# Other engines and row order for the ends of two weight loads, keys issued ahead of x, and a split projection, in a one-token decode layer

## Chip, cores and metric

The kernel runs on one core of a Trainium2 chip. The metric is the device time of one execution in microseconds (us). Several runs are taken of each kernel. The kernel before takes 196.8 to 197.0 us, depending on the set of runs. Differences of one per cent matter here, so each experiment was timed against the kernel before on the same chip, in alternating rounds.

## The reference, cut to what matters

Eight tokens go through attention over a cache (8 key heads, the last 1024 positions) and through a small MLP. A gate mixes the two.

```python
x: (8, 1, 448)   k_cache, v_cache: (8, 8, 4096, 256), last 1024 positions used
wq: (448, 4096)  wo: (4096, 448)   w1: (448, 1792)   w2: (1792, 448)
g = sigmoid((x * gate_w).sum(-1))
a = attention(x @ wq, k[..., -1024:, :], v[..., -1024:, :]) @ wo
b = gelu(layernorm(x) @ w1 + b1) @ w2 + b2
out = g * a + (1 - g) * b
```

About 78 MB have to be read for very little arithmetic. The 448 rows of `wq` and `w1` are 384 rows, which fill 128 partitions three times, and an end of 64 rows.

## The kernel before

Everything large streams through a ring of nine slots of 128 x 8192 elements. All of these loads are issued by the SP engine, in the order of a plan: keys 0, `w1`, `wq`, `w2`, then keys and values in turn, last `wo`. There are 16 steps of keys and values. The last `wo` part is split into three loads.

```python
wq_m = A_wq[0:DM, :].rearrange("(p r) n -> p (r n)", r=NR)      # 128 partitions
wq_t = A_wq[DM:D, :].rearrange("r (h n) -> (r h) n", h=2)       # end: 128 half rows
w1_m = B_w1[0:DM, :].rearrange("(p r) f -> p (r f)", r=NR)
w1_t = B_w1[DM:D, :].rearrange("r (h n) -> (r h) n", h=2)       # end: 128 half rows
...
x_sb = consts.tile([NB, D], BF16)
nc.sync.dma_start(x_sb[:], xf)     # x first on SP's queue
pump()                             # then the first nine loads of the plan
...
# the last steps (u is the last of 16)
values(u - 1)
...
finish(u - 1)
values(u)          # 32 matmuls: weights times values
finish(u)          # transposes the result into oT
for i in range(HPQ):               # row spread: 16 small matmuls into pp
    for m in range(HPQ):
        nc.tensor.matmul(pp[32*i : 32*i + 32, m], lhsT=ident[:, m::HPQ], rhs=oTv[:, i], ...)
nc.vector.tensor_copy(oP[:], pp[:]...)
for q in range(NHQ):               # projection: 128 matmuls with wo
    ...
nc.vector.scalar_tensor_tensor(res[:], in0=A_ps[:], scalar=gg_s[:, 0:1], in1=mixb[:], ...)
for i, (src, cols) in enumerate(quads(res)):     # four output stores
    eng = nc.sync if i % 2 == 0 else nc.scalar
    eng.dma_start(out_f[:, cols], src)
```

## Time and profile before

| kernel before | value | where it is read |
|---|---|---|
| time | 196.85 us median of 6 (196.59 to 197.06) | runs |
| bytes loaded on SP's queue | 77.67 MB at about 427 GB/s | page, queues and slices |
| share of DMA in the chain that ended last | 96% | page, chain |
| keys of step 14 begin | 160.78 us | timeline |
| compute's part of the projection ends | 190.05 us (187.00 + 3.05) | timeline |
| last `wo` part lands | just before 190.27 us | timeline, wait |
| the span ends | 195.0 us | page |

First the page of the profile of before, cut: the granted clock, the DMA share and the rate in forty slices of the span, then the DMA queues, then the chain that ended last.

```profile
PEclk9997566999999999999999999999999999999655
DMA  4999999999999999999999999999999999999940
GB/s 165 426 425 408 444 421 427 408 424 424 430 424 430 420 430 427 427 427 424 425 424 430 427 427 417 425 424 424 417 424 430 427 430 420 427 424 407 413 151 3
...
q1 hardware_dynamic: 6528, 77.67, 94.7%
q8 instruction: 18, 0.29, 0.6%
...
q14 instruction: 4, 0.03, 0.0%
...
DMA 96%; SPq 1%; issue 0%; PE 0%; DVE 0%
```

A DMA digit of 9 in 37 slices on end says that the loads never pause. Queue q1 is SP's. Two queues are of the kind "instruction", which I read as the program itself being fetched: 18 packets of 16 KB on q8, of 1.01 to 1.11 us each, and four of 8 KB on q14. The page counts them as a share of the same sixteen engines (0.6% for q8).

Next the table of stretches of before. The columns are the stretch, its length, the busy time of each compute engine with its number of instructions, the granted clock, the DMA share and the rate.

```profile
core 0: us, PE busy (x) PEld busy (x) DVE busy (x) ACT busy (x) POOL busy (x), PEclk, DMA share, GB/s
20.00:25.00 5.00, 4.59 (x137) 4.51 (x137) 1.55 (x7) 0.30 (x1) 0.00 (x0) 0.50 1.07 449
185.00:187.00 2.00, 1.14 (x20) 0.98 (x19) 0.65 (x2) 0.00 (x0) 0.00 (x0) 0.50 0.60 233
187.00:189.00 2.00, 2.00 (x88) 2.00 (x92) 0.00 (x0) 0.00 (x0) 0.00 (x0) 0.50 0.41 151
189.00:191.00 2.00, 1.41 (x52) 0.89 (x40) 0.32 (x1) 0.00 (x0) 0.00 (x0) 0.50 0.06 17
```

The end is not clean. The DMA share falls to 0.60, 0.41 and 0.06 over six microseconds, because the sixteen DMA engines finish at different times. A full load has sixteen completions in the trace, which I take for one per engine. Those of the last `wo` load spread over 4.6 us: seven come from 185.05 to 185.70 us, one at 187.28, seven from 188.16 to 188.67, and the last at 189.65.

The last microseconds of before in the timeline (start, duration, engine, source line, operation, and the idle time before it with what ended it):

```profile
187.00 3.05 PE L562 MATMUL A_ps<-slot,oP 128*8 128x112 bf16 x120 [0.55 <-DVE oP L555]
190.27 0.36 PE L562 MATMUL A_ps<-slot,oP 128*8 128x112 bf16 x8 [0.22 <-DMA slot<-in_A_wo_dram]
...
190.68 0.33 DVE L569 SCALAR_TENSOR_TENSOR res<-A_ps,gg_s,mixb 128x112 bf16<-128x112 f32 x1 [3.73 <-PE A_ps L562]
191.04 1.05 SPq L579 DMA_DIRECT2D out_dram<-res  x2
191.04 0.67 ACTq L579 DMA_DIRECT2D out_dram<-res  x2
```

The 120 matmuls that have their data end at 190.05, and the last eight wait for `wo` until 190.27. So loads and compute end within 0.3 us of each other. After the last sum (the DVE line) come the output stores: SP takes 1.05 us to issue its two, ACT 0.67.

One further line of the timeline of before marks how far the stream is near the end: the keys of step 14, which wait for their load.

```profile
160.78 1.51 PE L322 MATMUL ktp<-ident,slot 128*128 128x128 bf16 x24 [0.55 <-DMA slot<-in_A_k_cache_dram]
```

### The profile page before, as it was taken

The numbers are of one execution on the slowest core, as the hardware profiler recorded it, in microseconds if no ns is written. First come the engines' busy times: TensorE is split into PE (matmuls) and PEld (weight loads), VectorE is DVE, ScalarE is ACT, GpSimd is POOL, SyncE is SP. The second block draws the span as 40 slices with busy tenths as digits, with TensorE's granted clock in tenths as the row PEclk, the third lists the DMA queues.
The fourth block names the chain that finished last, engine by engine and source line by source line (L and its number), as shares of the span: only waits on it lengthen the run. The fifth ranks groups of instructions, "written<-read, shape, count | busy, mean of one in ns | idle before, by whom it ended". The sixth has DMA issues, their size and how long they took to land.

```text
span 195.0 us, 5167 instructions
## 1 busy us (share of the span) xinstructions
PE 148.3 (76%) x2318; PEld 110.5 (57%) x2318; DVE 112.6 (58%) x258; ACT 82.9 (43%) x101; POOL 0.9 (0%) x7
## 2 busy tenths in 40 slices
PE   1399967887778787878767878778787878994780
PEld 0399927755565656564636464647373737553570
DVE  7531342867575757575738484847575757777210
ACT  2362003636373727272708181818282828562000
POOL 1000000000000000000000000000000000000000
PEclk9997566999999999999999999999999999999655
DMA  4999999999999999999999999999999999999940
GB/s 165 426 425 408 444 421 427 408 424 424 430 424 430 420 430 427 427 427 424 425 424 430 427 427 417 425 424 424 417 424 430 427 430 420 427 424 407 413 151 3
DMA packets 6744, 78.02 MB, mean 400 GB/s; under 512 B 945, under 2 KB 1346, under 8 KB 1986
## 3 DMA queue, kind: packets, MB, share of 16 engines
q1 hardware_dynamic: 6528, 77.67, 94.7%
q8 instruction: 18, 0.29, 0.6%
q10 hardware_dynamic: 194, 0.02, 0.1%
q14 instruction: 4, 0.03, 0.0%
HBM read 77.68 MB, written 0.01 MB: 398 GB/s over the span
## 4 chain that ended last, share of the span: by engine, by line
DMA 96%; SPq 1%; issue 0%; PE 0%; DVE 0%
DMA slot<-in_A_k_cache_dram 58%; DMA slot<-in_A_v_cache_dram 20%; DMA slot<-in_A_wo_dram 10%; DMA slot<-in_A_wq_dram 7%; SPq L107 1%; SPq L123 1%; PE A_ps L562 0%; SPq L172 0%; DVE res L569 0%
## 5 line engine op out<-in xcount | busy, mean ns | idle before, releaser
L325 ACT COPY kt<-ktp 128x1024 bf16<-128x1024 bf16 x64 | 63.2, 1017 | 82.1 <-PE ktp L322 82.1
L322 PE MATMUL ktp<-ident,slot 128*128 128x128 bf16 x1024 | 71.2, 226 | 21.6 <-ACT kt L325 10.9
L322 PEld LDWEIGHTS <-slot 128*128 128x128 bf16 x1024 | 64.8, 103 | 28.4 <-issue 15.6
L327 DVE COPY kt<-ktp 128x1024 bf16<-128x1024 bf16 x64 | 41.3, 685 | 16.0 <-PE ktp L322 16.0
L360 PE MATMUL S_ps<-kt,qw 128*8 128x512 bf16 x256 | 32.4, 627 | 0.3 <-DVE qw L351 0.3
L372 DVE TENSOR_REDUCE nmx<-S_ps 128x1 f32<-128x1024 f32 x16 | 19.6, 1225 | 22.4 <-PE S_ps L360 22.4
L388 DVE STREAM_TRANSPOSE EB<-E 128x1024 bf16<-128x1024 bf16 x16 | 19.9, 1245 | 6.3 <-ACT E L380 6.1
L420 PE MATMUL PO<-slot,ET 128*8 128x256 bf16 x512 | 17.6, 282 | 6.1 <-DVE ET L401 6.1
L380 ACT ACTIVATE E<-S_ps,nmx 128x1024 bf16<-128x1024 f32 x16 | 17.9, 1120 | 2.4 <-DVE nmx L373 2.4
L420 PEld LDWEIGHTS <-ET 128*8 128x8 bf16 x512 | 11.4, 88 | 10.3 <-DVE ET L401 8.4
L360 PEld LDWEIGHTS <-qw 128*8 128x8 bf16 x256 | 7.3, 95 | 12.0 <-issue 10.4
L401 DVE CAST ET<-sm 128x256 bf16<-128x256 f32 x16 | 6.7, 417 | 0.5 <-PE sm L399 0.5
L396 PE MATMUL sm<-EB,perm 128*128 128x256 bf16 x16 | 4.4, 273 | 1.6 <-DVE EB L388 1.6
L399 PE MATMUL sm<-selr,ones_f 128*128 128x8 f32 x32 | 5.3, 237 | 0.0
L440 DVE CAST oT<-sm 128x16 bf16<-128x16 f32 x16 | 3.5, 221 | 2.8 <-PE sm L437 2.8
L399 PEld LDWEIGHTS sm<-selr,ones_f 128*128 128x128 f32 x32 | 4.8, 188 | 0.1
L562 PE MATMUL A_ps<-slot,oP 128*8 128x112 bf16 x128 | 3.4, 295 | 0.8 <-DVE oP L555 0.5
L339 PE MATMUL qt<-xT,slot 128*128 128x8 bf16 x128 | 3.6, 168 | 0.4 <-DVE z L470 0.4
L339 PEld LDWEIGHTS <-slot 128*128 128x128 bf16 x128 | 3.6, 104 | 0.4 <-issue 0.3
L562 PEld LDWEIGHTS <-oP 128*8 128x8 bf16 x128 | 2.9, 121 | 1.2 <-DVE oP L555 0.7
L470 DVE TENSOR_TENSOR z<-hT,b_sb 128x112 f32<-128x112 f32 x1 | 0.3, 275 | 5.5 <-PE hT L460 5.5
L380 ACT ACTIVATION_READ_ACCUMULATOR E<-S_ps,nmx 128x1 f32 x16 | 3.2, 202 | 0.0
(122 smaller groups left out, 71.9 us busy)
## 6 DMA issues: line engine op xcount, KB each, us to landing
slot<-in_A_v_cache_dram SPq DMA_DIRECT2D x16, 2048.0 KB, 38.9
slot<-in_A_k_cache_dram SPq DMA_DIRECT2D x15, 2048.0 KB, 39.4
slot<-in_A_wo_dram SPq DMA_DIRECT2D x3, 896.0 KB, 32.0
slot<-in_A_k_cache_dram SPq DMA_DIRECT2D x2, 1024.0 KB, 7.1
slot<-in_A_wq_dram SPq DMA_DIRECT2D x1, 2048.0 KB
slot<-in_B_w_dram SPq DMA_DIRECT2D x1, 1568.0 KB
slot<-in_B_w_dram SPq DMA_DIRECT2D x1, 1344.0 KB, 9.8
slot<-in_A_wq_dram SPq DMA_DIRECT2D x1, 1024.0 KB
```

Source lines behind the costliest of these rows:

```text
L322: nc.tensor.transpose(ktp[:, c, :], kn[:, o : o + P], ident[:])
L325: nc.scalar.copy(dst, ktp[:])
L327: nc.vector.tensor_copy(dst, ktp[:])
L339: nc.tensor.matmul(qt[:, k, :], lhsT=w[:, o + c : o + c + P], rhs=xT[:, r + half, :], start=(r == 0 and k == 0), stop=(r == NR), skip_grou ...
L360: nc.tensor.matmul(S_ps[32 * a : 32 * a + RQ, hf * CH * SK : (hf + 1) * CH * SK], lhsT=qw[:, j, b, half, a, :], rhs=KT[hf][:, j, :, a::QUA ...
L372: nc.vector.reduce_max(nmx[:], S_ps[:], axis=AXIS.X, negate=True)
L380: nc.scalar.activation(E[:], S_ps[:], ACT.Exp, bias=nmx[:], scale=1.0, accum_out=rowsum[:])
L388: nc.vector.transpose(EB[:].rearrange("p c r -> p (c r)"), E[:])
L399: nc.tensor.matmul(sm[:, NCK, :], lhsT=ones_f[:], rhs=selr[:], start=True, stop=True)
L401: nc.vector.tensor_copy(ET[:], sm[:, 0:NCK, :])
L420: nc.tensor.matmul(PO[32 * t : 32 * t + RQ, :], lhsT=ET[:, c, 0:RQ], rhs=vn[:, c * Dh : (c + 1) * Dh], start=(c < QUAD), stop=(c >= NCK - ...
L562: nc.tensor.matmul(dst, lhsT=oP[:, j, q, :], rhs=w[:, o + cols.start : o + cols.stop], start=(q == 0 and j == 0), stop=(q == NHQ - 1 and j ...
```

## The change

Three edits in one:

1. The ends of `wq` (512 KB) and `w1` (224 KB) are loaded as 64 full rows in partitions 0 to 63, not as 128 half rows in 128 partitions. The source is viewed as eight groups of eight rows, each group backwards. The load then runs on eight DMA engines (the load queue of after has 720 four-byte packets, taken for completion writes, against 736 in the run no_tails below, which keeps the old ends: eight fewer for each of the two). That each engine has one group of the view is how I laid out this load; the trace has no engine numbers and does not show it. The intent is to even out the finish of the engines, and to need fewer matmuls.
2. `x` goes to ACT's queue, so that the first keys are the first thing on SP's queue.
3. The row spread is cut in halves. The first half, and with it a part of the projection's preparation, moves ahead of the last value step, and a quarter of the projection is done before the second half.

```diff
-    wq_t = A_wq[DM:D, :].rearrange("r (h n) -> (r h) n", h=2)
+    wq_t = A_wq[DM:D, :].rearrange("(e j) n -> e j n", j=TE)[:, ::-1, :]    # TE = 8
-    w1_t = B_w1[DM:D, :].rearrange("r (h n) -> (r h) n", h=2)
+    w1_t = B_w1[DM:D, :].rearrange("(e j) n -> e j n", j=TE)[:, ::-1, :]
... (loader: destination t[0:64]; xT, yT and the matmuls of the end follow)
-    nc.sync.dma_start(x_sb[:], xf)
     pump()
+    nc.scalar.dma_start(x_sb[:], xf)
...
-    values(u)
-    finish(u)
-    (row spread of all heads, then the projection)
+    spread_rows(0, HALF)
+    values(u)
+    finish(u)
+    project(0)
+    spread_rows(HALF, NHQ)
+    for q in range(1, NHQ):
+        project(q)
```

More of the change, by code (lines that the diff above doesn't have):

```diff
@@ L51 @@
     NF = F // P
-    FH = F // 2
-    HH = HD // 2
+    TE = DT // 8
     QUAD = 4
@@ L116, in load @@
             for ap in pieces:
-                n = 1
-                for s in ap.shape[1:]:
-                    n *= s
-                dst = t[:, o : o + n]
-                if len(ap.shape) == 3:
-                    dst = dst.rearrange("p (a n) -> p a n", a=ap.shape[1])
-                nc.sync.dma_start(dst, ap)
+                n = ap.shape[-1]
+                rows = 1
+                for s in ap.shape[:-1]:
+                    rows *= s
+                nc.sync.dma_start(t[0:rows, o : o + n], ap)
                 o += n
@@ L191 @@
     nc.vector.memset(PO[:], 0.0)
-    NX = NR + 2
+    NX = NR + 1
     DQ = D // QUAD
@@ L200, in quads @@
         ]
-    xz = consts.tile([NB, 2, P], BF16)
-    yz = consts.tile([NB, 2, P], BF16)
-    nc.vector.memset(xz[:], 0.0)
-    nc.vector.memset(yz[:], 0.0)
+    xz = consts.tile([NB, DT], BF16)
+    yz = consts.tile([NB, DT], BF16)
     xT = consts.tile([P, NX, NB], BF16)
@@ L223, in transposed @@
             nc.tensor.transpose(tp[:, r, :], src[:, r:DM:NR], ident[:NB, :NB])
-        for h in range(2):
-            nc.tensor.transpose(tp[:, NR + h, :], srcz[:, h, :], ident[:NB, :NB])
-        nc.vector.tensor_copy(dst[:], tp[:])
-    for h in range(2):
-        nc.vector.tensor_copy(xz[:, h, h::2], x_sb[:, DM:D])
+        nc.vector.tensor_copy(
+            srcz[:].rearrange("b (e j) -> b e j", j=TE),
+            src[:, DM:D].rearrange("b (e j) -> b e j", j=TE)[:, :, ::-1],
+        )
+        nc.tensor.transpose(tp[0:DT, NR, :], srcz[:], ident[:NB, :NB])
+        nc.vector.tensor_copy(dst[:, 0:NR, :], tp[:, 0:NR, :])
+        nc.vector.tensor_copy(dst[0:DT, NR, :], tp[0:DT, NR, :])
     transposed(xT, x_sb, xz)
@@ L270, in norm_and_gate @@
         )
-        for h in range(2):
-            nc.vector.tensor_copy(yz[:, h, h::2], y_sb[:, DM:D])
         transposed(yT, y_sb, yz)
@@ L335, in query @@
             w, o = slot("wq", r // 2), (r % 2) * HD
+            kp = P if r < NR else DT
             for k in range(Hq * NJ):
                 col = (k // NJ) * Dh + (k % NJ) * P
-                half, c = divmod(col, HH) if r == NR else (0, col)
                 nc.tensor.matmul(
                     qt[:, k, :],
-                    lhsT=w[:, o + c : o + c + P],
-                    rhs=xT[:, r + half, :],
+                    lhsT=w[0:kp, o + col : o + col + P],
+                    rhs=xT[0:kp, r, :],
                     start=(r == 0 and k == 0),
@@ L446, in mlp_hidden @@
         w = slot("w1")
-        for r in range(NR):
-            o = r * F
+        for r in range(NR + 1):
+            kp = P if r < NR else DT
             for c in range(NF):
@@ L451, in mlp_hidden @@
                     hT[:, c, :],
-                    lhsT=w[:, o + c : o + F : NF],
-                    rhs=yT[:, r, :],
+                    lhsT=w[0:kp, r * F + c : (r + 1) * F : NF],
+                    rhs=yT[0:kp, r, :],
                     start=(r == 0 and c == 0),
-                    stop=False,
-                    skip_group_check=True,
-                )
-        for h in range(2):
-            for c in range(NF):
-                nc.tensor.matmul(
-                    hT[64 * h : 64 * h + 64, c, :],
-                    lhsT=w[:, NR * F + c : NR * F + FH : NF],
-                    rhs=yT[:, NR + h, :],
-                    start=False,
-                    stop=True,
+                    stop=(r == NR),
                     skip_group_check=True,
@@ L539, with spread_rows, project @@
     finish(u - 1)
-    values(u)
-    finish(u)
-    pp = ps_sm.tile([P, HPQ, NJ, NHQ, NB], F32, tag="sm", name="pp")
+    oP = consts.tile([P, NJ8, NHQ, NB], BF16)
     oTv = oT[:].rearrange("p (q i) j b -> p i j q b", i=HPQ)
-    for i in range(HPQ):
-        for m in range(HPQ):
-            nc.tensor.matmul(
-                pp[32 * i : 32 * i + 32, m],
-                lhsT=ident[:, m::HPQ],
-                rhs=oTv[:, i],
-                start=True,
-                stop=True,
-            )
-    oP = consts.tile([P, NJ8, NHQ, NB], BF16)
-    nc.vector.tensor_copy(oP[:], pp[:].rearrange("p m j q b -> p (m j) q b"))
-    for q in range(NHQ):
+    def spread_rows(q0, q1):
+        pp = ps_kt.tile([P, HPQ, NJ, q1 - q0, NB], F32, tag="ktp", name="pp")
+        for i in range(HPQ):
+            for m in range(HPQ):
+                nc.tensor.matmul(
+                    pp[32 * i : 32 * i + 32, m],
+                    lhsT=ident[:, m::HPQ],
+                    rhs=oTv[:, i, :, q0:q1, :],
+                    start=True,
+                    stop=True,
+                )
+        nc.vector.tensor_copy(
+            oP[:, :, q0:q1, :], pp[:].rearrange("p m j q b -> p (m j) q b")
+        )
+    def project(q):
         w = slot("wo", q - q % 2)
@@ L568 @@
                 )
+    HALF = NHQ // 2
+    spread_rows(0, HALF)
[5 more added lines that the diff above has]
+        project(q)
     nc.vector.scalar_tensor_tensor(
```

## The prediction

> **What bounds it now.** The loads. In the page's 40 slices the DMA row is at 9 throughout, 77.67 MB at about 427 GB/s; the chain of waits gives 96% of the span to DMA. But the last 5 us are not clean. In the table of stretches the DMA share is 1.02 at 180-185 us, then 0.60, 0.41 and 0.06 in the next three 2 us: the 16 DMA engines stop at different times. The trace's packets of the load queue end at about 185.2 us on seven engines, 187.4 on one, 188.2 to 188.8 on seven and 189.8 on one. The 18 instruction packets of 16 KB (about 1.06 us each) fit this: two on each of eight late engines, a third on the last.[...]
>
> A second limit runs beside it. In the timeline, keys 14 start on DMA at 160.78, then PE, ACT and DVE work in series to the last value step (182.25), finish, row spread and projection (120 matmuls, 187.00-190.05). The last 8 matmuls wait for wo until 190.23. So loads and compute end within 0.2 us of each other.
>
> **What changes.**
> 1. The tails of wq (512 KB) and w1 (224 KB) go to eight engines, not sixteen.[...] Those eight get 46 KB more, the others 46 KB less: at 427/16 GB/s, 1.73 us each way (estimate). I take it that the light eight are the early finishers (about 85%; the trace carries no engine numbers). Then ends become 186.9 (seven), 189.1 (the one at 187.4), 186.9 (seven), 188.0.
> 2. First keys lead the load queue: x's issue (0.73 to about 1.17 us) leaves it, so loads start 0.44 us earlier. x on ACT's queue is not critical.
> 3. 14 fewer hidden-layer matmuls, 2 fewer transposes, two memsets less; off the critical path (keys 1 wait for DMA at 31.36 anyway).
> 4. Projection: half the row spread before the last value step (delays it about 0.7 us: the oT copy, then 16 small matmuls); the rest hides its copies (0.32 + 0.55 us of PE idle before) behind projection. PE works at clock 0.5 there, so net about 0.1 us.
>
> **Sum.** The last wo landing moves from 190.23 to about 189.2 (0.44 + 0.6). Keys 14: the engine that is 1.4 us early now becomes the last, so they land only 0.1 to 0.5 us earlier, and compute follows: projection ends near 189.8. It ended at 190.63. Gain about 0.8 us, up to 2.2 if the intermediate engine is in the relieved half[...].
>
> **Predicted: 196.0 us, range 194.6 to 197.3.** Faster by over 2%: 0.05; within 2%: 0.92; slower: 0.03.
>
> **Right or wrong shows so.** Tail DMA share stays near 1 until about 186.5, then drops in under 2.5 us; first key packets start 0.4 us earlier; the projection's last matmuls no longer wait for wo but follow PE; keys 14 start within 0.5 us of 160.5; no PE idle from the copies after the last value step.
>
> **What would make it wrong.**[...] Early stages may suffer while the overloaded engines lag (wq lands later; query at 21.4).[...] Refill packets falling on other engines move the last landing by 1 us.

The sum came to a gain of about 0.8 us, with the end of the projection going from 190.63 to about 189.8 us, and of up to 2.2 us; the second case for the 2.2 us is cut, and so is a clock term of 1 to 2 us under what would make it wrong. For the landing of the last `wo` part, 0.6 is an estimate from the ends of the engines and the 1.73 us of step 1. Eight engines: if they were the late finishers, the end would slip by 1.3 us, to 198 us (an estimate: 1.73 less 0.44). How the 18 instruction packets (the "refill packets" of the last line) fall on the engines, and that they move the last landing by 1 us, are estimates from their count and the 1.06 us of one.

## The result, and the profile after

| | before | after |
|---|---|---|
| time, median of 6 runs | 196.85 us | 198.91 us |
| range | 196.59 to 197.06 | 198.27 to 200.39 |

The ratio after to before is 1.0111, with a 95% interval of 1.0075 to 1.0148. Ratios are the mean time of one kernel's fast runs over that of the other's fast runs of the same rounds, so they are not quite the ratio of the medians. The profiled run of after has a span of 196.5 us, against 195.0.

The page of after, the same lines as for before where they exist:

```profile
PEclk9997558699999999999999999999999999999755
DMA  5999999999999999999999999999999999999950
GB/s 210 412 377 407 268 392 427 422 424 427 420 427 424 427 424 427 427 427 424 430 429 420 427 424 430 424 425 420 430 430 430 424 430 427 427 428 404 404 215 13
...
q1 hardware_dynamic: 6368, 77.67, 95.3%
q8 instruction: 18, 0.29, 0.6%
...
DMA 83%; PE 9%; ACT 3%; DVE 2%; issue 1%; SPq 1%; ACTq 0%
```

The fifth number of the rate row is 268 GB/s, where before has 444. The DMA row still says 9 there. The engines are busy, but they move little: each packet takes longer. A busy share alone would have hidden it.

The table of stretches of after:

```profile
core 0: us, PE busy (x) PEld busy (x) DVE busy (x) ACT busy (x) POOL busy (x), PEclk, DMA share, GB/s
20.00:25.00 5.00, 1.98 (x69) 1.81 (x65) 0.49 (x2) 0.27 (x1) 0.00 (x0) 0.50 1.05 256
185.00:187.00 2.00, 1.69 (x32) 1.67 (x36) 0.58 (x3) 0.00 (x0) 0.00 (x0) 0.50 0.93 383
187.00:189.00 2.00, 1.48 (x29) 0.94 (x19) 0.46 (x2) 0.00 (x0) 0.00 (x0) 0.50 0.88 345
189.00:191.00 2.00, 2.00 (x68) 1.98 (x72) 0.23 (x2) 0.00 (x0) 0.00 (x0) 0.50 0.27 106
```

From 20 to 25 us the DMA share is 1.05 and the rate 256 GB/s, against 1.07 and 449 before. Near the end the DMA share stays high up to 189 us, so the loads end later.

In the table of waits of after, lines stand that before does not have, with PE waiting for these loads (total, number of times, longest):

```profile
PE qt L334 <- DMA slot<-in_A_wq_dram: 4.2, 2, 3.2
...
PE PO L415 <- DMA slot<-in_A_v_cache_dram: 1.1, 1, 1.1
```

The timeline of after, keys 14:

```profile
164.52 1.51 PE L317 MATMUL ktp<-ident,slot 128*128 128x128 bf16 x24 [0.52 <-DMA slot<-in_A_k_cache_dram]
```

Keys 14 start 3.74 us later than before (164.52 against 160.78). Then the end:

```profile
190.54 0.34 PE L532 MATMUL pp<-oT,ident 128*32 128x32 bf16 x16
...
190.70 2.52 PE L548 MATMUL A_ps<-slot,oP 128*8 128x112 bf16 x96
...
193.27 0.33 DVE L565 SCALAR_TENSOR_TENSOR res<-A_ps,gg_s,mixb 128x112 bf16<-128x112 f32 x1 [1.98 <-PE A_ps L548]
193.63 0.67 SPq L575 DMA_DIRECT2D out_dram<-res  x2
```

From keys 14 to the last sum, after needs 28.75 us (193.27 - 164.52) and before 29.90 (190.68 - 160.78). The rearranged end is therefore quicker, and the output stores are too: from the start of the last sum to the end of the span it is 3.2 us (196.5 - 193.27), against 4.3 before. So after loses 3.7 us early and wins back 2.2 us late (1.15 before the last sum, 1.1 behind it).

The packets of the trace show what was lost early. Two kinds of load overlap from 20 to 25 us: the end of `wq`, in packets of 8 KB, and `w2`, in packets of 12.25 KB. I tabulated their durations from the trace.

```
                         before         after
8 KB packet, normal      309 ns         309 ns
8 KB, end of wq          (none)         most take 600 to 650 ns
12.25 KB packet of w2    473 ns (all)   63 of 128 over 490 ns, 24 of them over 900 ns
3.5 KB, end of w1        (none)         35 of 64 over 150 ns, up to 292 ns (normal 140)
```

To have one number, I sum over all load packets between 10.5 and 38 us what each takes beyond the normal duration of its size, if that is over a tenth, and divide by 16 engines. Call it the loss per engine. It is 0.15 us before and 3.23 us after.

### The profile page after: what moved, and what is told of

Read it like the earlier page. It is cut to its first block, busy times and chain, and to the rows that moved or that the text cites. A ratio compares the mean times of both kernels' runs of the same rounds, so it can differ in the third digit from the quotient of the medians.

```text
span 196.5 us, 5165 instructions
## 1 busy us (share of the span) xinstructions
PE 146.3 (74%) x2318; PEld 109.2 (56%) x2318; DVE 112.4 (57%) x257; ACT 82.8 (42%) x101; POOL 0.8 (0%) x7
## 3 DMA queue, kind: packets, MB, share of 16 engines
q1 hardware_dynamic: 6368, 77.67, 95.3%
## 4 chain that ended last, share of the span: by engine, by line
DMA 83%; PE 9%; ACT 3%; DVE 2%; issue 1%; SPq 1%; ACTq 0%
DMA slot<-in_A_k_cache_dram 77%; DMA slot<-in_B_w_dram 5%; ACT kt L320 2%; PE S_ps L355 2%; PE ktp L317 2%; PE A_ps L548 2%; PE PO L415 1%; ACT E L375 1%; PE sm L432 1%; SPq L106 1%; DVE EB L383 1%; DVE nmx L367 1%; PE sm L394 0%; PE sm L391 0%; PE pp L532 0%
## 5 line engine op out<-in xcount | busy, mean ns | idle before, releaser
L317 PEld LDWEIGHTS <-slot 128*128 128x128 bf16 x1024 | 64.9, 103 | 29.1 <-issue 15.4
L415 PEld LDWEIGHTS <-ET 128*8 128x8 bf16 x512 | 12.0, 88 | 10.4 <-DVE ET L396 8.4
L334 PE MATMUL qt<-xT,slot 128*128 128x8 bf16 (+1 forms) x128 | 3.9, 167 | 4.6 <-DMA slot<-in_A_wq_dram 4.2
L334 PEld LDWEIGHTS <-slot 128*128 128x128 bf16 (+1 forms) x128 | 3.7, 104 | 4.8 <-DMA slot<-in_A_wq_dram 4.4
L346 DVE TENSOR_SCALAR qw<-qt 128x32 bf16<-128x32 f32 x8 | 0.9, 183 | 6.4 <-PE qt L334 6.4
L445 PE MATMUL hT<-yT,slot 128*128 128x8 bf16 (+1 forms) x56 | 3.6, 200 | 0.0
L445 PEld LDWEIGHTS <-slot 128*128 128x128 bf16 (+1 forms) x56 | 3.5, 160 | 0.0
```

The source lines that it names most:

```text
L317: nc.tensor.transpose(ktp[:, c, :], kn[:, o : o + P], ident[:])
L334: nc.tensor.matmul(qt[:, k, :], lhsT=w[0:kp, o + col : o + col + P], rhs=xT[0:kp, r, :], start=(r == 0 and k == 0), stop=(r == NR), skip_g ...
L415: nc.tensor.matmul(PO[32 * t : 32 * t + RQ, :], lhsT=ET[:, c, 0:RQ], rhs=vn[:, c * Dh : (c + 1) * Dh], start=(c < QUAD), stop=(c >= NCK - ...
L445: nc.tensor.matmul(hT[:, c, :], lhsT=w[0:kp, r * F + c : (r + 1) * F : NF], rhs=yT[0:kp, r, :], start=(r == 0 and c == 0), stop=(r == NR), ...
```

## The experiments

Three theories were tested on the early loss. **A**: the ends on eight engines cost all that was lost; if so, the question is what in them: the rows backwards (**R**), 64 partitions whoever writes them (**P**), or a run of eight neighbouring partitions written by one engine (**N**, later split into **M**, engines meeting on partitions, and **L**, the run itself). **B** is the rival of A: the rearranged end is to blame. For the gain at the end there are **S** (a store that meets an instruction packet) and **E** (the earlier start of the loads).

### no_tails: the other two edits alone

```diff
 (the kernel before, with edits 2 and 3 of the change, without edit 1)
```

> Keys first and the split projection alone; the ends of wq and w1 stay as 128 half rows on sixteen engines. Theory A (the eight-engine ends cost everything that was lost): faster than before, about 195.8 us: loads start 0.44 us earlier, and the projection's rearrangement, worth about 0.6 us after the keys of step 14 in the changed kernel's trace, comes on top. The stretch 20 to 25 us moves about 430 GB/s, not 256. Theory B (the loss comes from the end: the row spread ahead of the last value step delays it): slower than before, about 198 us.

Measured: 195.48 us (195.33 to 195.89), ratio 0.9934 (0.9920 to 0.9949). From 20 to 25 us the rate is 437 GB/s, and the loss per engine is 0.13 us. Edits 2 and 3 together are a gain, and theory B falls. This is the fastest of all kernels tried.

### tails_only: the first edit alone

```diff
 (the kernel after, with edits 2 and 3 taken back)
```

> Only the ends of wq and w1 as 64 rows on eight engines, with x first and the old projection. Theory A: about 200 us, that is the changed kernel plus the 0.44 us of the start and the 0.6 to 1 us of the projection; keys of step 1 land after 34.5 us, not at 31.4, and 20 to 25 us moves about 260 GB/s. Theory B: about 197 us, as before.

Measured: 201.51 us, ratio 1.0229 (1.0208 to 1.0250), loss per engine 3.67 us, 269 GB/s from 20 to 25 us; keys 1 start at 35.37 us. Edit 1 alone costs over two per cent. Theory A is right, and the time is 1.5 us above what I expected of it. The difference to after is 2.3 us of span (198.8 - 196.5): 0.9 at keys 14 (165.44 against 164.52), 0.65 between keys 14 and the last sum (29.40 against 28.75), and 0.8 after it.

### rows64_on16: forward rows, sixteen engines

```diff
-    wq_t = A_wq[DM:D, :].rearrange("(e j) n -> e j n", j=TE)[:, ::-1, :]
+    wq_t = A_wq[DM:D, :]
-    w1_t = B_w1[DM:D, :].rearrange("(e j) n -> e j n", j=TE)[:, ::-1, :]
+    w1_t = B_w1[DM:D, :]
```

> The changed kernel with the 64 rows of the ends read forward, which spreads them over sixteen engines, four rows each, into the same 64 partitions. Theory P (64 neighbouring partitions are what is slow[...], whoever writes): packets of 8 KB in that transfer still take about 600 ns, the core moves near half of its rate while they last, and the time stays within 1 us of the changed kernel, about 198 us. Theory N (an engine's run of eight neighbouring partitions collides with another engine's): [...]slow as well. Theory R (reading backwards is slow): packets take 309 ns, and the time is about 195.8 us.

Measured: 198.12 us, ratio 1.0055 (1.0038 to 1.0072), loss per engine 2.63 us. From 20 to 25 us the rate is 289 GB/s.

Nothing is read backwards here, the ends run on sixteen engines (6384 packets on the load queue, against 6368 in after: eight completions more for each of the two), and packets of the end still take about 600 ns. Theory R is out. P allows it, and so does N if runs of four can collide as well.

### runs_of_4: the same engines and bytes, runs of four partitions

```diff
-    TE = DT // 8
+    TE = DT // 16
-                nc.sync.dma_start(t[0:rows, o : o + n], ap)
+                    for h in range(2):
+                        nc.sync.dma_start(t[32 * h : 32 * h + 32, o : o + n], ap[8 * h : 8 * h + 8])
```

> The changed kernel with each end loaded by two transfers of 32 rows, each on eight engines in runs of four neighbouring rows, still read backwards; bytes for each engine are those of the changed kernel. Theory N (runs of eight neighbouring partitions make engines meet[...]): packets of 8 KB take 309 ns again, 20 to 25 us moves over 400 GB/s, about 196.5 us (what is left is the imbalance of bytes over the engines). Theory P (64 partitions[...]) and theory R (backwards): still 600 ns and about 198.5 us.

Measured: 195.87 us (195.54 to 196.36), ratio 0.9953 (0.9934 to 0.9972), loss per engine 0.15 us. The stretches of runs_of_4:

```profile
core 0: us, PE busy (x) PEld busy (x) DVE busy (x) ACT busy (x) POOL busy (x), PEclk, DMA share, GB/s
20.00:25.00 5.00, 3.54 (x91) 2.85 (x92) 1.21 (x10) 0.00 (x0) 0.00 (x0) 0.50 1.02 435
```

The rate is back (435 GB/s), the 8 KB packets take 309 ns again, and all 128 packets of `w2` are under 490 ns. The partitions 0 to 63 are the same, and so are the source, the backward order and the number of engines (6384 packets on the load queue, 16 more than in after: two loads more, with eight completions each). By its layout an engine only writes four neighbouring partitions per load, not eight. Theory P falls as I had put it. This edit is worth 3.0 us (198.91 - 195.87), close to the loss per engine that went with it (3.23 - 0.15 = 3.1).

### four_engines: runs of eight, but 32 partitions at a time

```diff
-                nc.sync.dma_start(t[0:rows, o : o + n], ap)
+                    for h in range(2):
+                        nc.sync.dma_start(t[32 * h : 32 * h + 32, o : o + n], ap[4 * h : 4 * h + 4])
```

> The changed kernel with each end loaded by two transfers of 32 rows, each on four engines in runs of eight neighbouring rows; an engine then writes the same eight-row runs, but within 32 partitions. Theory M (two engines must meet on one group of partitions[...]): 8 KB packets take 309 ns again, though four engines carry four times their share and the time is still about 198 us from that imbalance. Theory L (a run of eight is slow in itself): 8 KB packets take about 600 ns and the time is over 200 us.

Measured: 204.21 us, ratio 1.0366, loss per engine 5.98 us; the packets of the end are slow again (60 of them above 420 ns). My form of theory M, in which only engines of the same load can meet, and do not in these loads of 32 partitions, is refuted. (Four engines are by the layout, four groups of eight rows; no count of their completions is given.) Either a run of eight is slow in itself (L), or engines meet across loads: other engines are on `w2` at that time. The time does not tell them apart, as four engines also carry four times their share.

### upper_runs_of_4: runs of four, in the other half of the partitions

```diff
 (runs_of_4, and)
-                            t[32 * h : 32 * h + 32, o : o + n],
+                            t[64 + 32 * h : 96 + 32 * h, o : o + n],
 (the transposes and matmuls of the end use partitions 64 to 127)
```

> As runs_of_4 (two loads of 32 rows, eight engines, runs of four neighbouring rows), but into partitions 64 to 127, so with no run of eight anywhere. Theory M (what is slow is an engine writing to a group of partitions that another engine is writing at that time): [...]packets of both slow down again, 8 KB packets to about 600 ns, and the loads lose some 3 us per engine: about 198.5 us. Theory L (a run of eight neighbouring partitions is slow in itself): 309 ns and 195.9 us, as runs_of_4.

Measured: 199.33 us, ratio 1.0117 (1.0099 to 1.0134), loss per engine 3.70 us. The stretches of upper_runs_of_4:

```profile
core 0: us, PE busy (x) PEld busy (x) DVE busy (x) ACT busy (x) POOL busy (x), PEclk, DMA share, GB/s
20.00:25.00 5.00, 2.29 (x80) 2.12 (x77) 0.74 (x3) 0.30 (x1) 0.00 (x0) 0.50 1.03 239
```

There is no run of eight anywhere, and the rate is down to 239 GB/s, lower than in after. Only the destination moved by 64 partitions, and with it the matmuls of the end. So a run of eight is not needed for the loss: L as the only cause is out, and what M forecast for this run came true, though the ground for that forecast was not shown. Shown is that it matters which partitions the ends are written to: the same layout, with the same bytes in the same runs of four, is fast at partitions 0 to 63 (435 GB/s, a loss of 0.15 us per engine) and slow at 64 to 127 (239 GB/s, 3.70 us). The move cost about 3.2 us (ratios to before of 0.9953 and 1.0117).

M's reason, that two engines write to the same partitions at that time, is not shown, and the trace of four_engines speaks against it. There the end goes to 64 partitions in all. The engines that do not load it are on `w2` and then on keys 1, a load to all 128 partitions with one packet of 16 KB for each. From 24 to 31 us 74 of these packets start. They go to 74 partitions, so ten at least are not among the 64 of the end and should keep their speed. None does: all 74 take 1008 ns or more, against 614 normally. All engines are busy, and the core moves little more than half of its rate:

```profile
core 0: us, PE busy (x) PEld busy (x) DVE busy (x) ACT busy (x) POOL busy (x), PEclk, DMA share, GB/s
25.00:30.00 5.00, 0.00 (x0) 0.00 (x0) 0.00 (x0) 0.00 (x0) 0.00 (x0) 0.50 1.03 236
```

In after, too, the `w2` packets that start from 21 to 24.5 us, while the end of `wq` still loads, are slow without exception (37 of 37, 676 ns or more).

Why the place counts is open. My explanation rested on which engine writes which partitions in a full load, and that was not shown, as the trace has no engine numbers. How packets of other loads are slowed is open as well; that they are is measured, on `w2` in after (37 of 37 packets, 676 ns or more, against 473) and on keys 1 in four_engines (74 of 74, 1008 ns or more, against 614).

### w1_in_eights: only the smaller end in runs of eight

```diff
 (runs_of_4, and)
+                if len(ap.shape) == 3 and ap.shape[1] == 8:
+                    nc.sync.dma_start(t[0:DT, o : o + n], ap)
 (w1's end in groups of eight rows, wq's in groups of four)
```

> As runs_of_4, but the end of w1 (224 KB of the 736 KB) is one load of 64 rows in runs of eight again, and the end of wq stays in fours. If the loss grows with the bytes moved in eights, the packets lose 0.3 of the 3.1 us per engine that the changed kernel loses, about 1 us, and the time is about 196.8 us, between runs_of_4 (195.9) and the changed kernel (198.9). If wq alone matters, 195.9.

Measured: 197.15 us, ratio 1.0008 (0.9995 to 1.0021), loss per engine 0.98 us. The loss grows with the bytes: 224 of 736 KB would be 0.98 us of 3.23. The time is 1.3 us above runs_of_4 (1.1 by the two ratios to before, as the two were timed in different sets of runs), of which 0.8 come from the loss (0.98 - 0.15). SP issues 48 loads and stores here, as many as before, and its pair of output stores takes 1.05 us again, which is the next subject.

### keys_only: the second edit alone

```diff
-    nc.sync.dma_start(x_sb[:], xf)
     pump()
+    nc.scalar.dma_start(x_sb[:], xf)
```

> The kernel before with one edit: the first keys are issued on the load queue at once and x is loaded from ACT's queue. Theory S (the gain of this part is at the end: with one load fewer on its queue, the SP engine no longer meets an instruction refill between its two output stores): the first key packet starts 0.4 us earlier, but the last wo landing stays within 0.5 us of 190.2; from the end of the last sum to the end of the span takes 3.2 us, not 4.0; about 195.8 us. Theory E (the 0.44 us earlier start is all): 196.4 us, and the stretch after the last sum stays at 4.0 us.

Measured: 195.81 us (195.67 to 195.84), ratio 0.9946 (0.9933 to 0.9958). The end of the timeline of keys_only:

```profile
190.22 0.36 PE L562 MATMUL A_ps<-slot,oP 128*8 128x112 bf16 x8 [0.22 <-DMA slot<-in_A_wo_dram]
...
190.63 0.33 DVE L569 SCALAR_TENSOR_TENSOR res<-A_ps,gg_s,mixb 128x112 bf16<-128x112 f32 x1 [4.35 <-PE A_ps L562]
190.99 0.70 SPq L579 DMA_DIRECT2D out_dram<-res  x2
```

Keys 14 start 0.6 us earlier than before (160.17), but the last `wo` part lands at the same time (190.22 against 190.27), so the last sum gains only 0.05 us. The gain is behind it: SP's two stores take 0.70 us, not 1.05, and from the start of the sum to the end it is 3.2 us, not 4.3. That is theory S.

### proj_only: the third edit alone

```diff
 (the kernel before with spread_rows and project as in the change)
```

> The kernel before with one edit: the row spread in two halves and the first quarter of the projection ahead of the second. As compute ended 0.2 us before the last wo landing, the loads still decide: within 0.4 us of before, 196.4 to 197.0 us. If it is 196.0 or less, the projection was a limit of its own and theory S has to share its gain; if 197.5 or more, putting the row spread ahead of the last value step costs.

Measured: 196.88 us, ratio 0.9997 (0.9984 to 1.0011). The projection alone is worth nothing when the loads end last.

### one_more_on_sp: a failed test of S

```diff
 (no_tails, and)
-    nc.scalar.dma_start(b2_r[:], ...)
+    nc.sync.dma_start(b2_r[:], ...)
```

> The version with keys first and the split projection, and the load of the 448 biases b2 moved from ACT's queue to SP's, behind the first loads, so that SP issues as many loads as in the kernel before. Theory S: the second output store is issued late again and the stretch from the end of the last sum to the end of the span is back near 4.0 us, about 196.3 us. Theory E: unchanged at 195.5 us, with 3.2 us after the last sum.

Measured: 198.42 us. The test was spoiled: SP came to this load only after it had waited for ring slots, b2 was read at 43 us, and the MLP's second layer waited for it. The stretch in question did go up (SP's stores 1.07 us, 4.1 us from the sum's start to the end), but the time says nothing. It was repeated.

### b2_behind_w2: the repeat

```diff
 (no_tails, and)
+    def w2_and_b2(t):
+        rows_loader([w2_v])(t)
+        nc.sync.dma_start(b2_r[:], ...)
-    add(("w2",), rows_loader([w2_v]))
+    add(("w2",), w2_and_b2)
```

> The repeat of one_more_on_sp without its flaw (b2 came so late there that the second layer of the MLP waited for it): keys first and the split projection, ends of wq and w1 as before the change, and b2 loaded on SP's queue directly behind w2. Theory S: SP issues one load more than in no_tails, the pair of output stores takes 1.05 us to issue, not 0.70, and the stretch from the last sum's end to the span's end is back at 3.6 us or more, not 2.9; about 196.2 us. Theory E: 2.9 us and 195.5 us.

Measured: 196.40 us (196.19 to 196.85), ratio 0.9976 (0.9963 to 0.9989), against 0.9934 for no_tails. The end of the timeline of b2_behind_w2:

```profile
190.40 0.33 DVE L584 SCALAR_TENSOR_TENSOR res<-A_ps,gg_s,mixb 128x112 bf16<-128x112 f32 x1 [2.40 <-PE A_ps L567]
190.76 1.07 SPq L594 DMA_DIRECT2D out_dram<-res  x2
```

The last sum starts 0.4 us earlier than in no_tails (190.40 against 190.78), and the span still ends 0.4 us later (194.4 against 194.0). One small load more on SP's queue, some 180 us earlier, makes its output stores late. The trace shows the rest. Let N be the number of loads and stores that SP issues in all:

| kernel | N | gap between SP's two output stores, start to start | 8 KB instruction packet near the end |
|---|---|---|---|
| before, proj_only, tails_only, one_more_on_sp, b2_behind_w2, w1_in_eights | 48 | 0.74 to 0.78 us | before the last output packet is done |
| keys_only, no_tails, rows64_on16, after | 47 | 0.37 to 0.41 us | after it |
| runs_of_4, four_engines, upper_runs_of_4 | 49 | 0.38 to 0.39 us | 6 to 9 us before the stores (184.6 us in runs_of_4) |

In all six kernels with 48, the gap is twice as long. In before, the last output packet follows directly on that instruction packet (192.76 to 193.07 us, the output packet at 193.06). In before, 17 of the 18 instruction packets of 16 KB start from 18.64 to 184.82 us, in slices whose DMA digit is 9, so the loads go on beside them. One of 8 KB near the end stands out in the kernels with 48: it comes after both stores are issued and ahead of the last output packet. Shown is that in these kernels the number of SP's loads and stores decides (48 late, 47 and 49 not), as b2_behind_w2 put the delay back. That the 8 KB packet is SP's, and that the late issue of the second store belongs with it, is inferred from the counts; the trace does not name the owner.

### The sum

| part | worth | from |
|---|---|---|
| slow packets, from where the ends of `wq` and `w1` are written | +3.0 us | after minus runs_of_4 |
| ends on eight engines without that | +0.4 us | runs_of_4 minus no_tails (their intervals nearly touch) |
| keys first | -1.0 us | keys_only minus before |
| projection on top of keys first | -0.3 us | no_tails minus keys_only (intervals overlap) |
| sum | +2.1 us | measured: +2.06 |

As differences of medians, the four terms add up by construction: 3.04 + 0.39 - 0.97 - 0.33 = 2.13, up to the two values of before (196.85 and 196.78). What the table shows is the sizes.

## Why the prediction was wrong

The prediction was 196.0 us, 194.6 to 197.3, and 198.91 was measured. The change of 1.1% is within the 2% that I gave most of the chances, but in the other direction, and the time lies outside the range.

**The step that failed is step 1 of "What changes".** It put the ends' move to eight engines at plus or minus 1.73 us of bytes per engine, and the sum took "0.6" of gain at the last `wo` landing from it. It counted bytes per engine and nothing else; the duration of a packet was taken as fixed. The runs showed packets of twice the duration in these loads and in those beside them, 3.1 us per engine and 3.0 us of time, which no term of the sum stood for. Eight engines alone, with the packets at their normal duration, would not have cost this (runs_of_4). The list of what would make it wrong named late engines and instruction packets, and not this. Nor is it 64 partitions as such: runs_of_4 fills the same 64, 32 per load, at full rate (435 GB/s).

**The balance itself did not work either.** I took the eight engines that load the ends to be the early finishers. With the packets back at normal speed, in runs_of_4, the sixteen completions of the last `wo` load spread over 6.8 us, against 4.6 before and 5.2 in no_tails. Had the extra bytes gone to the early engines, the spread would have shrunk. Instead two engines are now 6.8 and 6.1 us ahead of the last. I have only a guess from these completions: that six of the eight relieved engines, and not all, carry instruction packets, and that two of the loaded ones do too. Keys 14 start 1.0 us later in runs_of_4 than in no_tails (161.33 against 160.31), where I had expected 0.3 from this step (1.4 ahead, 1.73 more bytes). The time differs by 0.4 us. The engine sets were not shown, as the trace has no engine numbers.

**Step 2, keys first, was right in its mechanism and wrong in where it pays.** The first key packets do start 0.42 us earlier in after, and keys 14 0.6 us in keys_only. The last landing did not move. The gain of 1.0 us came from SP's output stores, which I had not looked at, though the line of 1.05 us stood in the timeline beside ACT's 0.67.

**Step 3, the projection, was undersized.** I put it at 0.1 us. Where compute ends last, it is worth 0.65 us (29.40 us from keys 14 to the last sum in tails_only, 28.75 in after), but nothing where loads do (proj_only). Some of this can be the clock: the grant fell to half at 185.9 us in tails_only and at 184.7 in after, 20.5 and 20.2 us behind the start of keys 14.

Of the signs I named, three came true: first keys 0.4 us earlier, the projection's last matmuls no longer waiting for `wo`, and no idle PE for the copies after the last value step. The one that stood for the main claim failed: keys 14 within 0.5 us of 160.5 were at 164.52. The sign "DMA share near 1 for longer, then a quick drop" failed too. The share stays high longer only because the whole stream had slipped (0.88 at 187 to 189 us), and the drop is not quick: the completions of the last `wo` load spread over 6.8 us in after, against 4.6 before.

## What to carry to other kernels

A load's cost is not its bytes over its engines alone: where it wrote made 3.2 us. If a load covers only some partitions, try the same rows in another split and place (runs_of_4 against upper_runs_of_4). Look at the duration of single packets and at GB/s, not at the busy share, to see whether it worked. When a change at the front of a queue seems to pay, look at the last microseconds as well: one load more or less on a queue can make the final stores on it late, here by 0.8 to 1.1 us.
